# Weights read in steps of four columns, so that each partition loads four adjoining rows of w_out

## The chip, the cores and the metric

The kernel runs on one core of one Trainium2 chip. The metric is the device time of one execution in microseconds (us), lower is better. Engines are named as in the profile: PE is the matrix engine (PEld is its loading of weights), DVE the vector engine, ACT the scalar engine, POOL the general engine that also issues the loads which convert a type, and SP the engine that only issues transfers.

## The reference

Linear attention with a cosine weighting, and behind it a two-layer network with a squared ReLU. `q`, `k`, `v` are (8, 8, 576, 64) in float32, `moe_w_in` is (512, 2048), `moe_w_out` is (2048, 512).

```python
def phi(x, c, s):
    r = np.maximum(x, 0.0)
    return np.concatenate([r * c, r * s], axis=-1)
q_p = phi(q, cos_w, sin_w)
k_p = phi(k, cos_w, sin_w)
kv = np.einsum('bhsf,bhsd->bhfd', k_p, v)
z = np.sum(k_p, axis=2)
num = np.einsum('bhsf,bhfd->bhsd', q_p, kv)
den = np.einsum('bhsf,bhf->bhs', q_p, z)[..., None] + 1e-06
x = (num / den).transpose(0, 2, 1, 3).reshape(4608, 512)
h = x @ w_in
r = np.maximum(h, 0.0)
out = (r * r) @ w_out
```

The sum over the 2048 hidden units in the second product may be taken in any order, as long as the same unit is meant on both sides.

## The kernel before

Each of the eight batches has 576 tokens: four tiles of 128 (512 tokens, one "block" of the network) and a tail of 64. The eight tails make a ninth block. All products are in bfloat16 with sums in float32. For a block `m` the first product makes `gT[m]`, hidden units on the partitions (16 groups `hb` of 128 units), 512 tokens along the free side; ACT takes the ReLU out of PSUM (on-chip accumulator) and DVE squares. The second product takes slices of `gT` as weights and streams `w2sb`.

The weights stay on chip. `w1sb` is a tile of 128 partitions by 4 by 2048 (`kb`, hidden unit); `w2sb` is 128 by 16 by 512 (`hb`, output column). POOL loads each in four quarters: `load_w1(i, 4)` (L294 issues it) brings 512 columns of `w_in`, `load_w2(i, 4)` (L301) brings 512 rows of `w_out`. Both convert float32 to bfloat16 on the way. The quarters are called w1(0) to w1(3) and w2(0) to w2(3) below.

Where `w1sb` is used as weights of a matmul:

- `first_mm` (L712): the first product of block 0, 160 matmuls, in a hand-made order `FIRST_S` that begins with the quarter w1(0) for the first two token tiles; 64 of them are 128 wide, the others 256 wide;
- `unit_half` and `unit_mm` (L568, L584): the first product of block 1;
- `in_product` (L661): blocks 2 to 8, where the first product is made of seven half-size products in place of eight (a Strassen-like scheme). It takes quarters of `w1sb` or sums of them, `w1t[1]`, `w1t[2]`, `w1t[4]`, and `w1t[3]`, which lies in the place of a part of `w1sb`. DVE makes these sums in `w1_sum` (L619).

The second product is `first_out` (L737) for block 0, `out_pair` (L751) for block 1 and `product` (L850) for the others.

The order of everything is worked out on the host before the program is built. Each piece of work is handed to `Plan.add` with an engine, an assumed duration, what it reads and writes, and a due time; `Plan.order` then places the pieces in one list, and this list is the order in which instructions are written down. Each engine runs its own part of it strictly in that order. The reads and writes given to `Plan.add` only make this list. The waits that the chip really carries out are derived a second time, when the program is built: the framework looks at which bytes of a tile each instruction reads or writes, and in which order the instructions were written down. The loads of weights are given to the plan with fixed start times, 2.6 us apart:

```python
    plan_pool(2.6, lambda: load_w1(0, 4), [("w1", 0)])
    for i in range(1, 4):
        plan_pool(2.6, lambda i=i: load_w1(i, 4), [("w1", i)])
```

so in the written order the first matmuls of block 0 stand between the issues of w1(1) and w1(2), and more of them between w1(2) and w1(3). POOL's queue goes on, in this order, with q(1), w2(0), k(1), the tail of k(1), w2(1), v(1), the tail of v(1), w2(2), w2(3), where q(1), k(1), v(1) are the inputs of batch 1. The later batches are loaded by SP.

Of the kernel before, what the change touches and what calls it, by code (L numbers as in the profile page):

```python
# [158 lines left out]
def kernel(  # L159
# [10 lines left out]
    P = nc.NUM_PARTITIONS  # L170
# [118 lines left out]
    w1sb = wpool.tile([P, KB, DFF], BF16, name="w1sb")  # L289
    w2sb = wpool.tile([P, HB, DM], BF16, name="w2sb")  # L290

    def load_w1(i, n):
# [3 lines left out]
            in_=moe_w_in[:, f0:f1].rearrange("(kb p) f -> p kb f", p=P),  # L296
        )

    def load_w2(i, n):
        h0, h1 = i * HB // n, (i + 1) * HB // n  # L300
        nc.gpsimd.dma_start(  # L301
            out=w2sb[:, h0:h1, :],
            in_=moe_w_out[h0 * P : h1 * P, :].rearrange("(hb p) f -> p hb f", p=P),
        )


# [27 lines left out]
    def xT_of(b):  # L334
        return home(mlp, [P, 2, KB, W], "xT", b % 2)
# [225 lines left out]
    def x_block(m, kb):  # L561
        if m < B:
            return xT_of(m)[:, :, kb, :]
        return xT8[:, kb, :, :]

    def unit_half(m, hb, to, i):
        for kb in range(KB):
            nc.tensor.matmul(  # L568
                out=bank[to][:, i * W : (i + 1) * W],
                lhsT=w1sb[:, kb, hb * P : (hb + 1) * P],  # L570
                rhs=xT_of(m)[:, i, kb, :],
                start=(kb == 0),
                stop=(kb == KB - 1),
            )

    def unit_mm(m, hb, to):
        out_ = bank[to][:, :]
        rhs0 = x_block(m, 0)
        if m < B:
            out_ = out_.rearrange("p (i c) -> p i c", i=2)  # L580
        else:
            out_ = out_.rearrange("p (b c) -> p b c", b=B // 2)
        for kb in range(KB):
            nc.tensor.matmul(  # L584
                out=out_,
                lhsT=w1sb[:, kb, hb * P : (hb + 1) * P],
                rhs=x_block(m, kb),
                start=(kb == 0),
                stop=(kb == KB - 1),
            )  # L590
# [65 lines left out]
    def in_product(m, n, u, to):  # L656
        fresh, of = IN_PRODUCTS[n]
        lhs, rhs = of(m)
        for s in range(2):
            for kb in range(2):  # L660
                nc.tensor.matmul(  # L661
                    out=bank[to][:, s * W : (s + 1) * W],
                    lhsT=lhs[:, kb, (2 * u + s) * P : (2 * u + s + 1) * P],
                    rhs=rhs[:, kb, :],
                    start=(fresh and s == 0 and kb == 0),
                    stop=(kb == 1),
                    skip_group_check=True,
                )
# [37 lines left out]
    def first_mm(s, a, c0, step):  # L706
        half, hq = s // 4, s % 4
        for c in (c0,):
            for i in (2 * a, 2 * a + 1):
                hb = hq * 4 + i  # L710
                for kb in range(KB):
                    nc.tensor.matmul(  # L712
                        out=bank[2 * (FIRST_S.index(s) % 2) + i // 2][:, i % 2 * W + c : i % 2 * W + c + step],
                        lhsT=w1sb[:, kb, hb * P : (hb + 1) * P],
                        rhs=xT_of(0)[:, half, kb, c : c + step],
                        start=(kb == 0),
                        stop=(kb == KB - 1),
                    )
# [268 lines left out]
    def plan_unit(m, hb, to, due, halves=False):  # L987
        w1 = [("w1", hb // 4)]
        if halves:
            for h in range(2):  # L990
                add("PE", 4 * 0.1092, lambda h=h: unit_half(m, hb, to, h),
                    r=w1 + [("xT", m % 2, j) for j in (2 * h, 2 * h + 1)], w=[("bank", to)], due=due,
                    name=f"u{m}.{hb}.{h}")
        else:
            r = [("xT", m % 2, j) for j in range(J)] if m < B else [("xT8", i) for i in range(B // 2)]
            add("PE", 4 * 0.2158, lambda: unit_mm(m, hb, to), r=r + w1, w=[("bank", to)], due=due,
                name=f"u{m}.{hb}")
        add("ACT", cost("ACT", 512, "psum"), lambda: unit_relu(m, hb, to),
            r=[("bank", to)], w=[key for i in range(2) for key in g_keys(m, i, hb // HB2, (hb % HB2,))])
# [28 lines left out]
    def plan_gemm1_7(m, t, dt):  # L1028
# [19 lines left out]
        for u in range(HB2 // 2):  # L1048
# [5 lines left out]
            def prod(n, to):  # L1054
                add("PE", 4 * 0.1092, lambda u=u: in_product(m, n, u, to), r=reads[n], w=[("bank", to)],
                    due=t + (7 * u + STRIDE * c[0] + SHIFT) * dt, name=f"h{m}.{u}.{n}")
                c[0] += 1
# [210 lines left out]
    def plan_first(s):  # L1268
        n, half, hq = FIRST_S.index(s), s // 4, s % 4
        parts = ((0, P), (P, P)) if s in (0, 4) else ((0, W),)  # L1270
        for c0, step in parts:
            js = [2 * half + j for j in range(2) if c0 < (j + 1) * P and j * P < c0 + step]
            for a in range(2):
                to = 2 * (n % 2) + a
                add("PE", 8 * 0.1092 * step / W, lambda a=a, c0=c0: first_mm(s, a, c0, step),
                    r=[("xT", 0, j) for j in js] + [("w1", hq)], w=[("bank", to)], due=TM + (n + (a + c0 / P) / 4) * dt0)
        for a in range(2):
            to = 2 * (n % 2) + a
            add("ACT", 0.48, lambda a=a: first_relu(s, a), r=[("bank", to)],
                w=[("g", 0, half, hb // HB2, hb % HB2) for hb in range(4 * hq + 2 * a, 4 * hq + 2 * a + 2)])  # L1280
        add("DVE", 0.60, lambda: first_square(s),
            w=[("g", 0, half, hb // HB2, hb % HB2) for hb in range(4 * hq, 4 * hq + 4)])
# [14 lines left out]
    for half in range(2):  # L1297
        for i, e in enumerate(("DVE", "ACT")):
            js = slice(2 * i, 2 * i + 2)
            add(e, cost(e, FP, "cast"), lambda half=half, js=js, e=e: first_v(half, js, ENG[e]),  # L1300
                r=[("v", half)], w=[("v0", half, i)])
# [23 lines left out]

    plan_pool(2.6, lambda: load_main("q", 1, nc.gpsimd), [("q", 0), ("q", 1), ("q01",), ("q23",)])
    plan_pool(2.6, lambda: load_w2(0, 4), [("w2", 0)])
    plan_pool(2.75, lambda: load_main("k", 1, nc.gpsimd), [("k", 0), ("k", 1)])
    plan_pool(0.4, lambda: load_tail("k", 1, nc.gpsimd), [("kt", 1)])
    plan_pool(2.7, lambda: load_w2(1, 4), [("w2", 1)])  # L1330
    plan_pool(2.8, lambda: load_main("v", 1, nc.gpsimd), [("v", 0), ("v", 1)])
    plan_pool(0.4, lambda: load_tail("v", 1, nc.gpsimd), [("vt", 1)])
    for i in range(2, 4):
        plan_pool(2.6, lambda i=i: load_w2(i, 4), [("w2", i)])
# [6 lines left out]
    for hb in range(HB):  # L1341
        add("PE", 4 * 0.2158, lambda hb=hb: first_out(hb),
            r=[("g", 0, i, hb // HB2, hb % HB2) for i in range(2)] + [("w2", hb // 4)],
# [11 lines left out]
    for tt in range(J):  # L1355
        e = "ACT" if tt % 2 == 0 else "DVE"
        add(e, cost(e, 512, "psum"), lambda tt=tt, e=e: first_copy(tt, ENG[e]),
            r=[("bank", FIRST_Y[tt])], w=[("y", tt // 2, tt % 2)])
# [102 lines left out]
```

## Time and profile before

| | |
|---|---|
| median of 3 runs | 276.02 us (275.52 to 277.29) |
| profiled execution, its own time | 276.42 us |
| its span from first to last instruction | 274.6 us |
| PE busy | 265.0 us (96%) |
| PEld busy | 215.2 us (78%) |
| DVE busy | 225.9 us (82%) |
| ACT busy | 186.8 us (68%) |
| POOL busy | 15.2 us (6%) |
| mean granted clock of PE | 0.996 |

The busy time of PE is modelled: a matmul of 256 columns is shown as 273 ns long, while a run of them starts one every 109 ns. The span is shorter than the time by 1.8 us, which lie around the program. A line of the timeline gives start, length (both in us), engine, line of the code, operation, the tiles written and read with partitions and elements, and the number of equal instructions put together; in square brackets stands the idle time of the engine ahead of it and what ended that.

### The profile page before, as it was taken

The page shows a single profiled execution, that of the slowest core. Times are in us where ns is not written, and L with a number is a line of the kernel's source. Part 1 is how long each engine was busy: PE and PEld are TensorE (multiplying, and loading weights), DVE is VectorE, ACT ScalarE, POOL GpSimd, SP SyncE. Part 2 cuts the span into 40 slices and gives each one's busy share as a digit, 9 for nine tenths or more (in the row PEclk, how much of TensorE's full clock was granted, in tenths as well). Part 3 has the DMA queues.
Part 4 walks back from the last instruction along what each step waited for, and adds up shares of the span by engine and source line. Part 5 has one row for each costly group of instructions (what it writes and reads, how often), then busy time and mean ns, then how long its engine had stood idle before and what let it go on. Part 6 is the DMA issues. An engine that isn't in the chain of part 4 may idle for free.

```text
span 274.6 us, 6700 instructions
## 1 busy us (share of the span) xinstructions
PE 265.0 (96%) x2698; PEld 215.2 (78%) x2706; DVE 225.9 (82%) x450; ACT 186.8 (68%) x336; POOL 15.2 (6%) x29
## 2 busy tenths in 40 slices
PE   8989999999999999999999999999999999999993
PEld 3669856565478669899998889989988888888882
DVE  1865997947969999999999999999989974888911
ACT  3865671696689899898879997865646763464231
POOL 1563100000000000000000000000000000000022
PEclk9999999999999999999999999999999999999998
DMA  7999999999998979999999999985202100300134
GB/s 213 306 204 276 284 279 284 296 245 297 264 289 255 259 202 282 329 246 168 287 301 241 230 271 253 165 183 181 41 1 96 79 2 0 155 1 2 76 117 115
DMA packets 87006, 53.38 MB, mean 194 GB/s; under 512 B 56928, under 2 KB 83936, under 8 KB 86976
## 3 DMA queue, kind: packets, MB, share of 16 engines
q1 hardware_dynamic: 81504, 44.64, 63.4%
q0 software_dynamic: 5392, 8.26, 13.9%
q8 instruction: 21, 0.34, 0.5%
q10 hardware_dynamic: 80, 0.07, 0.1%
q14 instruction: 9, 0.07, 0.1%
HBM read 36.70 MB, written 9.44 MB: 168 GB/s over the span
## 4 chain that ended last, share of the span: by engine, by line
PE 80%; DMA 8%; DVE 3%; SPq 2%; issue 1%; ACT 1%; POOL 1%; POOLq 0%; DVEq 0%
PE bank L661 31%; PE bank L850 31%; DMA k<-in_k_dram 6%; PE bank L751 4%; PE bank L737 3%; PE abank L387 3%; PE bank L584 3%; PE abank L499 3%; DMA q<-in_q_dram 2%; DVE qp L345 1%; SPq L239 1%; ACT kp L341 1%; PE bank L568 1%; DVE gT L601 1%; SPq L249 1%
## 5 line engine op out<-in xcount | busy, mean ns | idle before, releaser
L661 PEld LDWEIGHTS <-w1sb 128*128 128x128 bf16 x448 | 43.3, 98 | 6.0
L661 PE MATMUL bank<-xT,w1sb 128*128 128x256 bf16 x336 | 47.8, 273 | 0.0
L850 PEld LDWEIGHTS <-gT 128*128 128x128 bf16 x448 | 43.3, 98 | 5.6 <-issue 0.6
L677 ACT ACTIVATE gT<-bank 128x512 bf16<-128x512 f32 x56 | 33.1, 600 | 16.9 <-PE bank L661 15.6
L850 PE MATMUL bank<-w2sb,gT 128*128 128x256 bf16 x336 | 41.9, 273 | 0.6 <-ACT ysb L761 0.6
L684 DVE TENSOR_TENSOR gT<-bank,qpTp 128x512 bf16<-128x512 f32 x56 | 36.7, 686 | 4.7 <-PE bank L661 3.7
L601 DVE TENSOR_TENSOR gT<-gT 128x2048 bf16<-128x2048 bf16 (+1 forms) x32 | 37.7, 1189 | 1.8 <-ACT gT L677 1.5
L1060 ACT COPY bank<-bank 128x512 f32<-128x512 f32 x56 | 31.4, 581 | 7.5 <-PE bank L661 7.0
L850 PEld LDWEIGHTS <-gs 128*128 128x128 bf16 x336 | 32.5, 98 | 3.8
L661 PEld LDWEIGHTS <-w1t 128*128 128x128 bf16 x336 | 31.9, 98 | 4.4
L661 PE MATMUL bank<-qpTp,w1t 128*128 128x256 bf16 x224 | 32.7, 273 | 0.0
L850 PE MATMUL bank<-w2t,gs 128*128 128x256 bf16 x224 | 27.6, 273 | 0.0
L1077 ACT COPY qpTp<-bank 128x512 f32<-128x512 f32 x28 | 16.1, 589 | 9.8 <-PE bank L661 5.6
L523 DVE TENSOR_TENSOR x<-abank,rden 128x512 bf16<-128x512 f32 x30 | 20.7, 691 | 1.0
L1148 DVE TENSOR_TENSOR ysb<-bank,y 128x512 f32<-128x512 f32 x14 | 9.7, 690 | 9.6 <-PE bank L850 8.3
L661 PE MATMUL bank<-xT,w1t 128*128 128x256 bf16 x112 | 16.8, 272 | 0.0
L661 PE MATMUL bank<-zeros,w1sb 128*128 128x256 bf16 x112 | 16.6, 273 | 0.0
L712 PE MATMUL bank<-xT,w1sb 128*128 128x256 bf16 (+1 forms) x160 | 15.5, 251 | 0.6 <-ACT gT L722 0.6
L341 ACT ACTIVATE qp<-q,sin_col 128x512 bf16<-128x512 f32 x23 | 16.1, 717 | 0.0
L784 POOL DMA_DIRECT2D out_dram<-ysb x4 | 2.4, 613 | 237.6 <-ACT ysb L1152 235.2
L341 ACT ACTIVATE kp<-k,cos_col 128x512 bf16<-128x512 f32 x18 | 12.6, 715 | 4.3 <-DMA k<-in_k_dram 4.3
L751 PE MATMUL bank<-w2sb,gT 128*128 128x512 bf16 x60 | 14.9, 379 | 0.5 <-DVE gT L601 0.3
(118 smaller groups left out, 423.5 us busy)
## 6 DMA issues: line engine op xcount, KB each, us to landing
out_dram<-ysb SPq DMA_DIRECT2D x16, 512.0 KB, 3.9
q<-in_q_dram SPq DMA_DIRECT2D x14, 512.0 KB, 6.3
v<-in_v_dram SPq DMA_DIRECT2D x14, 512.0 KB, 6.0
k<-in_k_dram SPq DMA_DIRECT2D x12, 512.0 KB, 6.7
w1sb<-in_moe_w_in_dram POOLq DMA_DIRECT2D x4, 512.0 KB, 9.3
w2sb<-in_moe_w_out_dram POOLq DMA_DIRECT2D x4, 512.0 KB, 17.5
k<-in_k_dram SPq DMA_DIRECT2D x1, 1024.0 KB, 5.6
q<-in_q_dram POOLq DMA_DIRECT2D x1, 1024.0 KB, 11.9
```

Of the source, the lines that this page charges most:

```text
L341: eng.activation(out=dst[ps, :, lo : lo + D], in_=src[ps], func=ACTF.Relu, scale=col[ps])
L523: nc.vector.tensor_tensor(out=x[:, a:z], in0=n4[:, :, :, 0:D].rearrange("p b (k l) d -> p b k l d", l=2), in1=rden[:, a:z] .rearrange("p b ...
L601: nc.vector.tensor_tensor(out=g, in0=g, in1=g, op=ALU.mult)
L661: nc.tensor.matmul(out=bank[to][:, s * W : (s + 1) * W], lhsT=lhs[:, kb, (2 * u + s) * P : (2 * u + s + 1) * P], rhs=rhs[:, kb, :], start= ...
L677: nc.scalar.activation(out=g_pair(m, i, j, u), in_=bank[to][:, :].rearrange("p (s c) -> p s c", s=2), func=ACTF.Relu,)
L684: nc.vector.tensor_tensor(out=g_pair(m, i, j, u), in0=bank[to][:, :].rearrange("p (s c) -> p s c", s=2), in1=in_five(u).rearrange("p (s c) ...
L712: nc.tensor.matmul(out=bank[2 * (FIRST_S.index(s) % 2) + i // 2][:, i % 2 * W + c : i % 2 * W + c + step], lhsT=w1sb[:, kb, hb * P : (hb + ...
L751: nc.tensor.matmul(out=bank[LAST_Y[s_]][:, :], lhsT=gT_of(m)[:, hb, tt * P : (tt + 1) * P], rhs=w2sb[:, hb, :], start=(hb == 0), stop=(hb ...
L850: nc.tensor.matmul(out=bank[to][:, s * DM2 : (s + 1) * DM2], lhsT=lhs[:, hb, s * P : (s + 1) * P], rhs=rhs[:, hb, :], start=(fresh and hb ...
L1060: add("ACT", psum, lambda: nc.scalar.copy(out=bank[b][:, :], in_=bank[a][:, :]), r=[("bank", a)], w=[("bank", b)])
L1077: add("ACT", psum, lambda u=u, Y=Y: nc.scalar.copy(out=in_five(u), in_=bank[Y][:, :]), r=[("bank", Y)], w=five)
L1148: lambda: nc.vector.tensor_tensor(out=y_view(m, i, cc), in0=half_bank(a), in1=five_of(m)[:, :, :], op=ALU.add),
```

## The change

`load_w2` gives each partition four rows of `w_out` that lie one behind the other, one stretch of 8 KB in memory, where before it took four rows that lie 128 rows apart, four stretches of 2 KB. With that, the hidden unit at partition `p` of group `hb` is another one: within each quarter of 512 units it is unit `4 p + hb mod 4`. So that the first product makes the same units in the same places, its weights are taken from `w1sb` in steps of four columns: `cols(hb)` is a slice with a step of 4 elements (8 bytes) in place of 128 adjoining columns. The loading of `w1sb`, the sums of the weights, and the number, shapes and order of the instructions stay.

```diff
+    RUN = 4
+
+    def cols(hb):
+        c0 = hb // RUN * RUN * P + hb % RUN
+        return slice(c0, c0 + RUN * (P - 1) + 1, RUN)
+
     def load_w2(i, n):
         h0, h1 = i * HB // n, (i + 1) * HB // n
+        assert h1 - h0 == RUN
         nc.gpsimd.dma_start(
             out=w2sb[:, h0:h1, :],
-            in_=moe_w_out[h0 * P : h1 * P, :].rearrange("(hb p) f -> p hb f", p=P),
+            in_=moe_w_out[h0 * P : h1 * P, :].rearrange("(p r) f -> p r f", r=RUN),
         )
...
 # unit_half, unit_mm, first_mm (L568, L584, L712)
-                lhsT=w1sb[:, kb, hb * P : (hb + 1) * P],
+                lhsT=w1sb[:, kb, cols(hb)],
...
 # in_product (L661)
-                    lhsT=lhs[:, kb, (2 * u + s) * P : (2 * u + s + 1) * P],
+                    lhsT=lhs[:, kb, cols(2 * u + s)],
```

More of the change, by code (lines that the diff above doesn't have):

```diff
@@ L585, in unit_mm @@
                 out=out_,
-                lhsT=w1sb[:, kb, hb * P : (hb + 1) * P],
+                lhsT=w1sb[:, kb, cols(hb)],
                 rhs=x_block(m, kb),
@@ L713, in first_mm @@
                         out=bank[2 * (FIRST_S.index(s) % 2) + i // 2][:, i % 2 * W + c : i % 2 * W + c + step],
-                        lhsT=w1sb[:, kb, hb * P : (hb + 1) * P],
+                        lhsT=w1sb[:, kb, cols(hb)],
                         rhs=xT_of(0)[:, half, kb, c : c + step],
```

## The prediction

> **What bounds the kernel now.** I read the busy shares first, then the costliest groups, the timeline of the first 25 us, the landing of the loads, and the instruction lists of the two builds side by side.
>
> ```profile
> PE 265.0 (96%) x2698; PEld 215.2 (78%) x2706; DVE 225.9 (82%) x450; ACT 186.8 (68%) x336; POOL 15.2 (6%) x29
> L661 PEld LDWEIGHTS <-w1sb 128*128 128x128 bf16 x448 | 43.3, 98 | 6.0
> L661 PE MATMUL bank<-xT,w1sb 128*128 128x256 bf16 x336 | 47.8, 273 | 0.0
> ```
>
> PE runs nearly from end to end, so any microsecond in which PE stands still is lost: nothing later has slack to give it back. Weight loads lie beside the matmuls (a 256-wide matmul starts every 109 ns, the load is shown as 98 ns).
>
> The timeline of PE and POOL in the first stage, where the weights arrive:
>
> ```profile
> 10.60 3.15 POOL L294 DMA_DIRECT2D w1sb<-in_moe_w_in_dram  x4
> 17.67 0.61 PE L712 MATMUL bank<-xT,w1sb 128*128 128x128 bf16 x8
> 18.12 0.61 PE L480 MATMUL bank<-ident,qp 128*128 128x128 bf16 x8
> 18.56 0.61 PE L712 MATMUL bank<-xT,w1sb 128*128 128x128 bf16 x8
> 19.01 0.41 PE L499 MATMUL abank<-kvz,qpTp 128*128 128x65 bf16 x8
> 19.25 2.10 PE L712 MATMUL bank<-xT,w1sb 128*128 128x128 bf16 x24
> 21.66 1.91 PE L712 MATMUL bank<-xT,w1sb 128*128 128x256 bf16 x16
> 22.70 0.70 POOL L249 DMA_DIRECT2D vt<-in_v_dram  x1 [1.38 <-DMA w1sb<-in_moe_w_in_dram]
> 25.29 0.76 POOL L301 DMA_DIRECT2D w2sb<-in_moe_w_out_dram  x1 [1.89 <-DMA w1sb<-in_moe_w_in_dram]
> ```
>
> POOL issues all four quarters of w_in back to back from 10.60. PE starts L712 at 17.67, while w1(2) and w1(3) are still under way; POOL's later waits end at 22.70 and 25.29 because these two have just landed. Landing by issue, from the view of the transfers in 10.5 to 11.3 us and in 11.3 to 12.1 us (last column: median us from issue to landing):
>
> ```profile
> w1sb<-in_moe_w_in_dram POOLq DMA_DIRECT2D x1, 512.0 KB, 5.8
> w1sb<-in_moe_w_in_dram POOLq DMA_DIRECT2D x2, 512.0 KB, 7.1
> ```
>
> w1(0): 10.60 + 5.8 = 16.4. The second row is the mean of 5.8 and w1(1)'s own, so 8.4; issued at 11.49, w1(1) lands at 19.9. w1(3) lands at about 25.0, just ahead of the wait that ends at 25.29.
>
> **The change, part by part.**
>
> *The order* of instructions is the same on all five engines. *The waits are not.* With a step of four, the framework no longer sees that `cols(hb)` of one quarter stays clear of the other quarters. The build of the changed kernel has, new:
> - PE: the second weight load of the first L712 group (17.67) waits for w1(1); the second load of the next one (18.56) waits for w1(2); the second load of the group at 21.66 waits for w1(3). Before, PE met these waits only where the quarter was needed.
> - POOL: the issue of w1(2) waits until PE has finished the first L712 group; the issue of w1(3) until PE has finished the run that starts at 19.25. Before, neither waited.
> - Near 71 us: `w1_sum(3)` on DVE waits for four L661 matmuls, and a weight load two matmuls on waits for that sum.
>
> So two loads that were issued ahead now stand behind PE, and PE behind them; q(1), w2(0), k(1) and all else in POOL's queue stand behind both.
>
> *Step 1, first stall.* The group of 17.67 goes on at 19.9: seven matmuls 56 ns apart (eight L480 take 0.45) and the length of the last, 0.22, end it at 20.5.
>
> *Step 2, w1(2).* Issued at 20.6. How long does such a load take alone? Upper bound 5.8 (w1(0), beside other loads until about 12.5). Lower bound: the 2.6 us that one quarter lands behind another (22.70 to 25.29), plus the 2.4 us of the shortest POOL transfer of the page (128 KB), less 0.3 for its own data at that pace: 4.7. I take 5.5, nearer to the row of the same transfer. It lands at 26.1; PE has stood since about 21.1.
>
> *Step 3, the clock.* Rows on what PE does after standing still (windows; behind PE's and the other engines' busy times come granted clock, share and rate of the transfers; then weight loads of the start):
>
> ```profile
> 269.00:270.00 1.00, 0.92 (x9) 0.58 (x6) 0.00 (x0) 0.42 (x2) 0.26 (x1) 1.00 0.77 176
> 272.00:273.00 1.00, 0.00 (x0) 0.00 (x0) 0.00 (x0) 0.00 (x0) 0.00 (x0) 0.84 0.50 147
> 273.00:274.60 1.60, 0.00 (x0) 0.00 (x0) 0.00 (x0) 0.00 (x0) 0.00 (x0) 0.50 0.00 0
> 5.43 0.15 PEld L369 LDWEIGHTS <-zeros 128*128 128x128 bf16 x1 [0.27 <-issue]
> 5.86 0.15 PEld L369 LDWEIGHTS <-zeros 128*128 128x128 bf16 x1 [0.28 <-issue]
> 6.29 3.20 PEld L369 LDWEIGHTS <-zeros 128*128 128x128 bf16 x15 [0.28 <-issue]
> ```
>
> The last matmul ends at 269.9 and the clock halves at 272.7, 2.8 us later. At the start PE works from 1.2 at one load per 0.43 us, and from 6.3 at one per 0.21: 5.1 us of work at half speed. A stall of 5 us is over the 2.8, so PE comes back at half speed for about 5.1 us. [...]
>
> *Step 4, w1(3).* From the freed load to the end of the run at 19.25 + 2.10 = 21.35, PE needed 2.7 us (18.6 to 21.35), 2.4 of it matmuls; at half speed 5.0. So POOL issues w1(3) at 31.1, and it lands at 36.6. PE stands for another 4 to 5 us ahead of the group that stood at 21.7.
>
> *Step 5, the loss at this point:* 36.6 - 21.7 = 14.9 us. The clock is low once more for 5.1 us; the timeline shows PE without a gap from 21.7 to 36.5 (L712, then L737), so half of that is lost: 2.6 us.
>
> *Step 6, what comes back.* w1(3) lands 11.6 us later than before (36.6 against 25.0) and the queue behind it follows at its old spacing, so q(1), k(1), w2 are late by 11.6, PE by 14.9 to 17.5. They are no longer what PE waits for. The gap of 0.56 us ahead of PE's L712 at 37.07 (ACT late, because k(1) landed at 33.95) goes: -0.6.
>
> *Step 7, near 71 us:*
>
> ```profile
> 71.42 1.04 PE L661 MATMUL bank<-xT,w1sb 128*128 128x256 bf16 x8
> 71.67 1.22 DVE L619 TENSOR_TENSOR w1sb<-w1sb 128x2048 bf16<-128x2048 bf16 x1
> 74.48 1.04 PE L751 MATMUL bank<-w2sb,gT 128*128 128x512 bf16 x4 [0.29 <-DVE gT L601]
> ```
>
> The sum starts when four of the eight L661 are done (72.0) and ends at 73.3; the other matmuls end their starts at 73.8, eight L751 at 216 ns follow to 75.5, where before PE went on at 74.48 after a wait that is then covered: +1.1 us.
>
> *Step 8, w2's longer stretches.* A quarter lands about 2.6 us behind the one before. Were w2 faster, the gain would be covered, since by step 6 these loads lead PE by 3 us or more; at most the 0.6 already counted. POOL's issue (0.77 us) is off the path. Without that cover it could give some tenths.
>
> *Step 9, weights read with a step.* No row shows one. Lower end: 65-wide matmuls start every 33 ns (40 of L387 in 1.31 us), so a packed load needs no more than that of PE; a stepped one like it is hidden at no cost. Upper ends: if the shown 98 ns were all occupied, the 64 matmuls that are 128 wide lose 98 - 56 = 42 ns each, 2.7 us; if a load took four packed ones (four times the bytes are spanned), 132 ns, 904 matmuls of 256 lose 23 ns and the 64 lose 76: 25.7 us. The nearest row is the other form of load: 16 of 64 columns start within 0.22 us (L499, 100.05), 15 ns each, 30 for 128 columns. I take nothing.
>
> *Sum:* 14.9 + 2.6 - 0.6 + 1.1 = 18.0, on the profiled execution's own 276.4 (span 274.6 and 1.8 around it): 294.4. Its own time is 0.4 over the median of 276.0; the forecast for the median is 294.0.
>
> **Rivals.**
> 1. *The clock does not fall* in these stalls. For: the profile's clock row reads 1.00 wherever PE had gaps of 1 us. Against: 2.8 us at the end. Then step 4 is 2.7 us (28.8), w1(3) lands at 34.4, the loss is 12.7 and no 2.6: 276.4 + 12.7 + 0.5 = 289.6; with 4.7 us a load, 288.
> 2. *Stepped weights are slow as well:* 2.7 to 25.7 us more, 297 to 320. For: 78% of the span has weights loading. Against: the pitches of step 9. [...]
> 3. *Not slower:* the new waits are over when an engine reaches them, and only longer stretches of w2 remain: the 0.6 of step 6, 275.8. It needs w1(2) to land within 0.3 us of an issue that can't come before 18.3, and the shortest transfer took 2.4; from a wait of a further microsecond it turns round.
>
> **How the numbers follow.** Forecast 0.64, rival 1 0.15, rival 2 0.18, rival 3 0.03. The range goes from rival 1 with loads of 4.7 us and an earlier w1(1), 287, to rival 2's smaller prices above the forecast with loads of 5.8, 300; the far end of rival 2 and rival 3 are left out. Changes within 1% are about what a measurement here can't tell from none: slower 0.97, same 0.02, faster 0.01.
>
> **What would show it.** Right: POOL's four L294 in three pieces (about 10.6, 20.6, 31); PE gaps ahead of L712 ended by w1sb landings, 2, 5 and 4 to 5 us long; a clock below 1 in 20 to 42 us; from 80 us on the same pitch. Wrong: L661 starts further apart than 109 ns (rival 2), a full clock (rival 1), or L294 still in one piece (rival 3).

## The result and the profile after

The changed kernel takes 293.76 us (median of 4 runs, 292.69 to 294.11), where the kernel before took 275.77 us beside it (4 runs, 275.22 to 277.29): 1.065 times as long, with a 95% interval of 1.062 to 1.067. The profiled execution's own time is 294.11 us, its span 292.3 us, 17.7 us over the 274.6 before. The nine new lines of code shift what follows `load_w1`: L661 of before is L670 now, L712 is L721, L480 is L489, L737 is L746, L568 is L577, L619 is L628, L751 is L760; `load_w1` stays L294.

The page of the changed kernel, with the busy shares, the granted clock in 40 slices of 7.3 us each (in tenths), and the groups of the first product:

```profile
PE 270.6 (93%) x2698; PEld 230.0 (79%) x2706; DVE 225.6 (77%) x450; ACT 186.7 (64%) x336; POOL 14.4 (5%) x29
PEclk9975769999999999999999999999999999999999
L670 PEld LDWEIGHTS <-w1sb 128*128 128x128 bf16 x448 | 48.6, 114 | 3.0 <-DVE w1sb L628 1.5
L721 PE MATMUL bank<-xT,w1sb 128*128 128x256 bf16 (+1 forms) x160 | 20.9, 299 | 11.4 <-DMA w1sb<-in_moe_w_in_dram 11.4
```

The last line has the loss in it: 11.4 us in which PE's first product waits for landings of `w_in`, where before none of PE's waits was for `w_in`. The clock row falls in slices three to six (14.6 to 43.8 us) and nowhere else. The weight loads are shown 114 ns long in place of 98, but a 256-wide matmul still starts every 109 ns: eight L670 matmuls stand in the timeline with a length of 1.04 us, as eight L661 did.

The timeline of PE and POOL in the first stage and up to where block 0 is done (the square brackets are the idle time ahead and what ended it):

```profile
10.41 1.70 POOL L294 DMA_DIRECT2D w1sb<-in_moe_w_in_dram  x2
19.41 0.94 PE L721 MATMUL bank<-xT,w1sb 128*128 128x128 bf16 x7 [1.86 <-DMA w1sb<-in_moe_w_in_dram]
20.64 0.74 POOL L294 DMA_DIRECT2D w1sb<-in_moe_w_in_dram  x1 [8.54 <-PE bank L721]
26.06 0.94 PE L721 MATMUL bank<-xT,w1sb 128*128 128x128 bf16 x7 [4.75 <-DMA w1sb<-in_moe_w_in_dram]
31.15 0.74 POOL L294 DMA_DIRECT2D w1sb<-in_moe_w_in_dram  x1 [9.76 <-PE bank L721]
36.67 3.39 PE L721 MATMUL bank<-xT,w1sb 128*128 128x256 bf16 x15 [4.77 <-DMA w1sb<-in_moe_w_in_dram]
53.81 1.04 PE L721 MATMUL bank<-xT,w1sb 128*128 128x256 bf16 x8
```

Read it as a ladder. POOL issues two quarters and then waits 8.54 us for PE; PE waits 4.75 us for the quarter that POOL could issue only then; POOL waits 9.76 us for PE again, and PE 4.77 us for the last quarter. Before, the four issues stood in one line (10.60, x4). On each rung of the last two, PE resumes 5.4 and 5.5 us after the issue: the time of one load alone.

Windows of the same stretch (busy time of PE, PEld, DVE, ACT, POOL; then granted clock, share and GB/s of the transfers):

```profile
18.00:20.00 2.00, 0.59 (x6) 0.59 (x7) 0.29 (x1) 0.00 (x0) 0.00 (x0) 0.53 0.12 17
26.00:28.00 2.00, 1.94 (x23) 1.94 (x24) 0.46 (x3) 0.60 (x1) 0.00 (x0) 0.50 0.00 0
32.00:34.00 2.00, 0.00 (x0) 0.00 (x0) 0.79 (x2) 0.00 (x0) 2.00 (x3) 1.00 0.50 55
34.00:36.00 2.00, 0.00 (x0) 0.00 (x0) 0.00 (x0) 0.00 (x0) 2.00 (x4) 0.79 1.26 215
40.00:42.00 2.00, 2.00 (x22) 2.00 (x21) 0.42 (x1) 0.60 (x1) 0.40 (x1) 0.50 1.03 305
```

In 26 to 28 and in 40 to 42 us PE is at work almost without a break, at half the clock.

Where the 17.7 us of span arose is seen from how much later the same work starts in the changed kernel:

| work | before | after | later by |
|---|---|---|---|
| group that waits for w1(3) (L712, L721) | 21.66 | 36.67 | 15.0 |
| eight transposes behind the half clock (L480, L489) | 28.91 | 46.38 | 17.5 |
| last eight of block 0 (L712, L721) | 37.07 | 53.81 | 16.7 |
| first L661, L670 of the next product | 71.42 | 88.13 | 16.7 |
| the eight L661, L670 after the eight L751, L760 | 75.35 | 92.99 | 17.6 |
| end of the span | 274.6 | 292.3 | 17.7 |

(The 36.67 is the first matmul that waited, the second of its group; the group's first, at 31.51, had not.) The first two rows are the ladder and its half clock, the third gives 0.7 us back, the fifth is the place where `w1_sum(3)` stands:

```profile
88.13 0.71 PE L670 MATMUL bank<-xT,w1sb 128*128 128x256 bf16 x5
88.77 1.23 DVE L628 TENSOR_TENSOR w1sb<-w1sb 128x2048 bf16<-128x2048 bf16 x1 [0.31 <-PE bank L670]
90.05 0.52 PE L670 MATMUL bank<-xT,w1sb 128*128 128x256 bf16 x3 [1.21 <-DVE w1sb L628]
92.99 1.04 PE L670 MATMUL bank<-qpTp,w1t 128*128 128x256 bf16 x8
```

The eight L670 are cut into five and three, and between them PE waits 1.21 us for DVE's sum, which itself could start only when some of these matmuls had read the old weights.

### The profile page after: what moved, and what is told of

It reads as the page before. It is cut to its first block, busy times and chain, and to the rows that moved or that the text cites. A ratio compares the mean times of both kernels' runs of the same rounds, so it can differ in the third digit from the quotient of the medians.

```text
span 292.3 us, 6700 instructions
## 1 busy us (share of the span) xinstructions
PE 270.6 (93%) x2698; PEld 230.0 (79%) x2706; DVE 225.6 (77%) x450; ACT 186.7 (64%) x336; POOL 14.4 (5%) x29
## 3 DMA queue, kind: packets, MB, share of 16 engines
q0 software_dynamic: 3856, 8.26, 12.4%
## 4 chain that ended last, share of the span: by engine, by line
PE 85%; DMA 7%; issue 4%; POOL 1%; DVE 1%; SPq 1%; ACT 0%; POOLq 0%
PE bank L670 30%; PE bank L859 29%; PE bank L721 5%; PE bank L746 5%; PE bank L760 5%; DMA w1sb<-in_moe_w_in_dram 5%; PE bank L593 4%; PE abank L396 3%; PE abank L508 3%; DMA v<-in_v_dram 2%; PE bank L577 1%; PE bank L489 1%; POOL w1sb L294 1%; PE bank L554 0%; DVE w1sb L628 0%
## 5 line engine op out<-in xcount | busy, mean ns | idle before, releaser
L670 PEld LDWEIGHTS <-w1sb 128*128 128x128 bf16 x448 | 48.6, 114 | 3.0 <-DVE w1sb L628 1.5
L670 PE MATMUL bank<-xT,w1sb 128*128 128x256 bf16 x336 | 48.0, 273 | 1.2 <-DVE w1sb L628 1.2
L686 ACT ACTIVATE gT<-bank 128x512 bf16<-128x512 f32 x56 | 33.0, 600 | 16.9 <-PE bank L670 15.6
L693 DVE TENSOR_TENSOR gT<-bank,qpTp 128x512 bf16<-128x512 f32 x56 | 36.6, 682 | 4.7 <-PE bank L670 3.8
L670 PEld LDWEIGHTS <-w1t 128*128 128x128 bf16 x336 | 36.0, 114 | 1.1
L670 PE MATMUL bank<-qpTp,w1t 128*128 128x256 bf16 x224 | 32.8, 273 | 0.0
L721 PE MATMUL bank<-xT,w1sb 128*128 128x256 bf16 (+1 forms) x160 | 20.9, 299 | 11.4 <-DMA w1sb<-in_moe_w_in_dram 11.4
L721 PEld LDWEIGHTS <-w1sb 128*128 128x128 bf16 x160 | 17.0, 128 | 13.6 <-DMA w1sb<-in_moe_w_in_dram 12.2
L731 ACT ACTIVATE gT<-bank 128x512 bf16<-128x512 f32 x16 | 9.1, 596 | 20.2 <-PE bank L721 20.2
L526 DVE TENSOR_SCALAR den<-abank 128x8 f32<-128x8 f32 x34 | 5.4, 159 | 19.4 <-PE abank L508 15.9
L670 PE MATMUL bank<-xT,w1t 128*128 128x256 bf16 x112 | 16.8, 273 | 0.0
L670 PE MATMUL bank<-zeros,w1sb 128*128 128x256 bf16 x112 | 16.6, 273 | 0.0
```

Source lines behind the costliest of these rows:

```text
L670: nc.tensor.matmul(out=bank[to][:, s * W : (s + 1) * W], lhsT=lhs[:, kb, cols(2 * u + s)], rhs=rhs[:, kb, :], start=(fresh and s == 0 and ...
L686: nc.scalar.activation(out=g_pair(m, i, j, u), in_=bank[to][:, :].rearrange("p (s c) -> p s c", s=2), func=ACTF.Relu,)
L693: nc.vector.tensor_tensor(out=g_pair(m, i, j, u), in0=bank[to][:, :].rearrange("p (s c) -> p s c", s=2), in1=in_five(u).rearrange("p (s c) ...
L721: nc.tensor.matmul(out=bank[2 * (FIRST_S.index(s) % 2) + i // 2][:, i % 2 * W + c : i % 2 * W + c + step], lhsT=w1sb[:, kb, cols(hb)], rhs ...
```

## The experiments

The theory is that of the prediction: the stepped reads of one large tile make the framework put in waits that the data don't need; they tie two loads and PE to each other, and with the idle time the clock halves (0.50 in the windows above). The rivals are that the stepped weight loads cost time themselves, and that the other half of the change, `w2`'s longer stretches, does something. Each experiment takes one of these away or has it alone.

**split_tiles: the change kept, the tile taken apart.** Each quarter of `w_in` gets its own tile, so that a stepped slice can't reach into another quarter. The sums of the weights become two instructions each.

```diff
-    w1sb = wpool.tile([P, KB, DFF], BF16, name="w1sb")
+    w1q = [wpool.tile([P, KB, FQ], BF16, name=f"w1sb{i}") for i in range(4)]
-            out=w1sb[:, :, f0:f1],
+            out=w1q[i][:, :, :],
-                lhsT=w1sb[:, kb, cols(hb)],
+                lhsT=w1q[hb // RUN][:, kb, cols(hb % RUN)],
...
-        nc.vector.tensor_tensor(out=w1t[n], in0=in0, in1=in1, op=op)
+        for x in range(2):
+            nc.vector.tensor_tensor(out=to(x), in0=in0(x), in1=in1(x), op=op)
```

> Both parts of the change stay (steps of four, four adjoining rows of w_out), but each quarter of w_in has a tile of its own, so that no load or matmul waits for another quarter; each of the four weight sums is written as two instructions. If the added waits are the whole loss: POOL's four loads of w_in in one piece from about 10.5 us, the clock at full speed in 18 to 42 us, no PE wait on a landing of w_in over 0.3 us, and the time of before plus 0 to 1 us for the four more DVE instructions: 275.5 to 277.5 us. If stepped weights cost by themselves: the loss stays in the stages of L712 and in_product; 2.7 us (279) if the 64 matmuls of 128 columns wait for loads that are now shown as 114 to 128 ns, more if the 256-wide ones start over 109 ns apart.

Measured: 275.82 us (12 runs) against 275.6 for the kernel before (23 runs), a ratio of 1.0003 (0.9987 to 1.002); span 274.0 us, mean clock 0.999. POOL's and PE's timeline, and the group of the stepped loads:

```profile
10.52 3.23 POOL L295 DMA_DIRECT2D w1sb<-in_moe_w_in_dram  x4
36.34 1.04 PE L726 MATMUL bank<-xT,w1sb 128*128 128x256 bf16 x8
```

```profile
L675 PEld LDWEIGHTS <-w1sb 128*128 128x128 bf16 x448 | 48.7, 113 | 1.6
```

The four issues are in one piece again, and PE nowhere waits for `w_in`. The loads are as stepped as in the changed kernel, and shown as long (113 ns), yet the loss is gone. So the loss is in the waits, and stepped weights cost nothing that this comparison could see; nor do they where matmuls are 128 columns wide, since runs of 8 and 24 L726 take 0.45 and 2.11 us as before. The second line answers to the 37.07 of before: its 0.56 us of idle time ahead is gone.

**steps_alone and rows_alone: the two halves of the change.** The first is the changed kernel with the old `load_w2`; the second is the kernel before with the new one. In both, the hidden units of the two products no longer correspond; the work is the same in amount.

```diff
# steps_alone, against the changed kernel
-            in_=moe_w_out[h0 * P : h1 * P, :].rearrange("(p r) f -> p r f", r=RUN),
+            in_=moe_w_out[h0 * P : h1 * P, :].rearrange("(hb p) f -> p hb f", p=P),
# rows_alone, against the kernel before
-            in_=moe_w_out[h0 * P : h1 * P, :].rearrange("(hb p) f -> p hb f", p=P),
+            in_=moe_w_out[h0 * P : h1 * P, :].rearrange("(p r) f -> p r f", r=4),
```

> The changed kernel with the old load of w_out (rows 128 apart); the steps of four stay, so the hidden units of the two products do not match. Waits theory: all of the loss, 293 to 295 us, with the same three PE stalls. If the load of w_out has a part in it, the time moves off 293.8 by that part.

> Before, with only the load of w_out changed to four adjoining rows; the weights of the first product stay packed, so the hidden units of the two products do not match. Waits theory: 275.2 to 276.4 us, no different from before, since w2 leads PE. If the longer stretches are worth something: k(1) lands 0.2 to 0.6 us earlier than 33.95 and the time falls by as much. If the load of w_out were part of the loss: several us slower.

Measured: steps_alone 293.94 us (292.55 to 295.47), ratio 1.0655 (1.0612 to 1.0698), with 12.3 us of PE's waits for `w_in` in three pieces. rows_alone 275.4 us (275.21 to 276.84, 12 runs), ratio 0.9992 (0.9975 to 1.0009). All of the loss is in the steps. The longer stretches do work in the queue: q0 carries 3856 packets in the changed kernel where it carried 5392, and in rows_alone k(1) lands 0.9 us sooner after the first weight load's issue (22.5 us in place of 23.4), so that PE's wait of 0.56 us goes. The 0.9 is more than the 0.2 to 0.6 that was expected. In the time this can't be told from nothing.

**loads_first: the ladder without its rungs.** The issues of all four quarters are written down ahead of the first matmul. POOL then has nothing of PE's to wait for; PE's own false waits stay, and become one wait for the last of the four landings.

```diff
-    plan_pool(2.6, lambda: load_w1(0, 4), [("w1", 0)])
+    plan_pool(2.6, lambda: [load_w1(i, 4) for i in range(4)], [("w1", 0)])
     for i in range(1, 4):
-        plan_pool(2.6, lambda i=i: load_w1(i, 4), [("w1", i)])
+        plan_pool(2.6, lambda: None, [("w1", i)])
```

> The changed kernel with all four loads of w_in written down ahead of the first matmul that uses w_in. POOL no longer waits for PE; PE waits once, for all four quarters. If it is the chain of PE and POOL waiting for each other in turn that costs: one PE stall from 17.4 to about 25.0 (7.5 us), half clock for some 5 us after it (2.5 us), the sum near 71 us (1.1), less 0.6: 286 to 288 us. If POOL's waits do not matter: 293 to 295 us.

Measured: 285.91 us (285.09 to 286.26), ratio 1.0353 (1.0315 to 1.0391); a tenth under the expected range. POOL's loads stand in one piece at 10.32, and PE's timeline has a single stall:

```profile
24.68 0.91 PE L721 MATMUL bank<-xT,w1sb 128*128 128x128 bf16 x7 [7.03 <-DMA w1sb<-in_moe_w_in_dram]
```

So the 18 us are two things: 293.76 - 285.91 = 7.9 us because POOL's issues wait for PE (with the half clock that this adds), and some 10 us because PE waits for quarters that it doesn't yet need. The second is made up of the 7.0 us, half of the 5.7 us at half clock that follow (2.9), the 0.9 at the sum, less the 0.7 that comes back: 10.1, against a measured 10.3 (285.91 against 275.6).

**filled: the clock by itself.** The waits stay, but PE gets matmuls on zeros ahead of the waiting groups (7, 20 and 20 of them, into banks that are free then), so that it never stands long. They add work and change no result that is used.

```diff
+    FILL = {(0, 1, 0): (7, 0), (0, 1, P): (20, 0), (1, 0, 0): (20, 1)}
...
     def first_mm(s, a, c0, step):
         half, hq = s // 4, s % 4
+        fill(*FILL.get((s, a, c0), (0, 0)))
```

> The changed kernel with matmuls on zeros written ahead of the three waiting groups of L712 (7, 20 and 20, each 512 columns wide), so that PE works while it would stand; nothing reads their results. If the halved clock is part of the loss: granted clock 1.00 from 15 to 45 us, POOL's third w_in load issued about 2.4 us earlier relative to the second (the work between the stalls at full speed), no half-speed stretch after the last stall (2.6 us): 288 to 290 us. If the clock costs nothing: 293 to 295 us, or more, by the added matmuls.

Measured: 289.14 us (288.64 to 290.18), ratio 1.0497 (1.0478 to 1.0516). PE still stands 0.35, 0.88 and 2.02 us, and the clock stays full from 15 to 45 us; one of the windows:

```profile
24.00:28.00 4.00, 3.12 (x43) 2.57 (x42) 1.06 (x3) 1.14 (x2) 0.00 (x0) 1.00 0.35 57
```

Doing more work makes the changed kernel faster by 293.76 - 289.14 = 4.6 us. It acts twice: the work after the last stall runs at full speed (the 15 matmuls behind it take 1.83 us in place of 3.39), and the third and fourth issue stand 8.3 us apart (20.30 and 28.59) in place of 10.5, because the matmuls between them do too. The price of the clock may be somewhat higher than this difference: in filled the last load took 6.6 us from its issue (28.59) to PE's resumption (35.21), in place of 5.5, and no run shows why.

**first_plain: the place at the sum by itself.** Of the product that reads `w1sb` just ahead of `w1_sum(3)`, the first two groups take packed columns, so that they read only the quarter they need. These groups compute other hidden units.

```diff
-                    lhsT=lhs[:, kb, cols(2 * u + s)],
+                    lhsT=lhs[:, kb, (2 * u + s) * P : (2 * u + s + 1) * P]
+                    if (m, n) == (2, 1) and u < 2
+                    else lhs[:, kb, cols(2 * u + s)],
```

> The changed kernel, but the first two groups of in_product (block 2, first product, the eight matmuls ahead of the third weight sum) take packed columns, so their hidden units do not match. The wait between these matmuls and the sum near 71 us (88 us in the changed kernel) goes. By the prediction's step 7: 1.1 us less than the changed kernel, 292.4 to 293.0 us, and no PE wait on w1_sum. If that stall was covered by the wait behind it: 293.5 to 294 us.

Measured: 292.8 us (290.8 to 294.57, 6 runs), ratio 1.063 (1.06 to 1.066). The runs spread over 3.8 us, so the median's distance of 1.0 us from the changed kernel says little, and so does its place in the expected range. The trace says more:

```profile
85.75 1.04 PE L670 MATMUL bank<-xT,w1sb 128*128 128x256 bf16 x8
89.67 1.04 PE L670 MATMUL bank<-qpTp,w1t 128*128 128x256 bf16 x8
```

The eight are in one piece, and the next eight follow 3.92 us later; in the changed kernel it was 4.86 (88.13 to 92.99), in the kernel before 3.93 (71.42 to 75.35). The false wait at the sum costs 0.94 us.

**bursts: what a stepped load needs of PE when little hides it.** In the kernel before, the last 8 of the 28 matmuls on zeros at the start are replaced by four bursts of 16 matmuls of only 64 columns, with weights that are packed (L372) or read in steps of two (L376), four (L380) and eight (L384).

```diff
+        warm(20)
+        packed(16)       # lhsT=probe[:, 0:P]
+        step_two(16)     # lhsT=probe[:, 0:255:2]
+        step_four(16)    # lhsT=probe[:, 0:509:4]
+        step_eight(16)   # lhsT=probe[:, 0:1017:8]
```

> Before, with the last 8 of the 28 warming matmuls replaced by four bursts of 16 matmuls of 64 columns on zeros, whose weights are packed, or in steps of two, four and eight columns, each burst on a line of its own. It measures what a stepped load occupies. If a stepped load costs only its added length (114 against 98 ns, overlapped): all bursts start one matmul every 30 to 35 ns. [...] Time within 1 us of before.

Measured (one run: 275.64 us), PE's timeline:

```profile
7.75 0.63 PE L372 MATMUL abank<-zeros,gT 128*128 128x64 bf16 x16
8.22 0.63 PE L376 MATMUL abank<-zeros,gT 128*128 128x64 bf16 x16
8.69 0.70 PE L380 MATMUL abank<-zeros,gT 128*128 128x64 bf16 x16
9.22 1.14 PE L384 MATMUL abank<-zeros,gT 128*128 128x64 bf16 x16
```

From start to start of the bursts, 16 matmuls take 0.47, 0.47 and 0.53 us: 29, 29 and 33 ns each. The last burst's length of 1.14 us, less the 0.16 us that its last matmul is shown to last beyond its turn in the first burst (0.63 - 0.47), gives about 61 ns; the next matmul in the timeline starts at 10.19, 0.97 us after the burst, which gives the same. So a step of four bf16 needed at most 33 ns per load of 128 columns, far below the 109 ns of a 256-wide matmul and the 56 ns of a 128-wide one; a step of eight needed some 60. The first three bursts are at or under the 30 to 35 ns of a load that costs only its added length, the fourth does not; why, no run shows.

**wide_steps: steps of eight where PE is busiest.** split_tiles, with the weights of three of the products (336 loads) read in steps of eight from the tiles of the sums; these products compute other hidden units.

```diff
# against split_tiles, for products 5, 6 and 3
+    def wide_cols(h):
+        return slice(h, h + 8 * (P - 1) + 1, 8)
...
-    lhsT=lhs((2 * u + s) // RUN)[:, kb, cols((2 * u + s) % RUN)],
+    lhsT=lhs[:, kb, wide_cols(2 * u + s)],
```

> The split kernel, with the weights of the three products that use sums of w_in taken in steps of eight columns (16 bytes), the others in steps of four; the hidden units of these products do not match. If loads in steps of eight stay hidden beside 256-wide matmuls (109 ns apart): 275.4 to 276.4 us, and their shown length tells the slope: 98 packed, 114 at four, 130 to 140 at eight. If they take over 109 ns of the loading path: 336 loads times the excess, several us slower.

Measured: 276.33 us (275.91 to 276.94, 10 runs), ratio to the kernel before 1.0032 (1.0022 to 1.0043); the loads are shown longer than a 109 ns matmul turn:

```profile
L678 PEld LDWEIGHTS <-w1t 128*128 128x128 bf16 x336 | 38.8, 145 | 1.0
```

If 145 ns were occupied, 336 loads would lose (145 - 109) x 336 = 12 us. Between half a microsecond (276.33 against split_tiles' 275.82, which ran on another occasion) and 0.9 us (against the 275.44 of the kernel before beside it) is there, so the shown length of a weight load is not its price.

## Why the prediction was right

The forecast was 294.0 us, and 293.76 was measured; the loss of 18.0 on the profiled execution came out as 17.7 of span. By its steps:

- *The order and the waits.* Right. POOL's four L294 stand in three pieces, and PE's three stalls end with landings of `w1sb`. That the stepped reads of a single tile are the cause, and not the step as such, is shown by split_tiles. How the framework works out the reach of a stepped slice was not looked at; only the waits it made were. What stands ahead of the prediction says that it looks at which bytes an instruction reads; for a stepped slice the waits it made cover quarters of which not a byte is read.
- *Step 1.* PE went on at 19.4, not 19.9, but at half speed: its seven matmuls took 0.94 us. The two errors cancelled, and POOL's issue came at 20.64 (forecast 20.6).
- *Step 2.* 5.4 and 5.5 us for a load alone, forecast 5.5. It was chosen between 4.7 and 5.8 by the row of the same transfer, and that row came nearer.
- *Step 3.* The clock did halve, but the rule behind the forecast was wrong. It took 2.8 us of standing for the fall and 5.1 us of work for the return, each from one instance. In the traces of the changed kernel, loads_first and first_plain the clock changed at instants that lie 3.41 us or whole multiples of it apart, and fell 0.6 to 5.2 us after the last matmul (worked out in the last section). Here it fell some 0.6 us after the last matmul ahead of the first stall (17.55; the mean of 0.53 in 18 to 20 us means half clock from about 18.1 on), in a stall of 1.86 us that the forecast took for harmless. The return took 5.7 and 5.3 us of work. That this is so near the 5.1 is in part luck: in first_plain, whose code is the same in this stage, the clock stayed full in the first stall and the returns took 2.8 and 3.4 us. Its profiled execution of 290.8 us, with the 0.9 of step 7 added, is 2.4 us under the changed kernel's 294.11.
- *Step 4.* 26.06 to the issue at 31.15 is 5.1 us, forecast 5.0; the last landing at 36.67, forecast 36.6.
- *Step 5.* 15.0 us and 17.5 - 15.0 = 2.5, forecast 14.9 and 2.6.
- *Step 6.* Forecast -0.6, measured -0.7: the gap ahead of the last L721 is gone, and nothing behind the late loads in POOL's queue made PE wait. rows_alone and split_tiles, in which PE is not late, lose the gap too, and k(1) lands 0.9 us earlier in both (in split_tiles at 33.06). steps_alone, in which PE is late and `w_out` is loaded as before, has no such gap either: no L721 waits for ACT among its waits of 0.3 us and more. So PE's lateness takes the gap away by itself, as forecast, and the longer stretches alone would have done it as well.
- *Step 7.* Forecast 1.1, measured 0.93, by the table and by first_plain. The mechanism was the one described. Of the small error, 0.1 is in the forecast's own sum (75.5 - 74.48 is 1.0, not 1.1); the rest is that PE had issued five of the eight matmuls ahead of its wait, where the forecast left four of them behind it.
- *Step 8.* Nothing that can be measured, as forecast: rows_alone has 0.9992.
- *Step 9.* Nothing, as forecast: 114 ns shown, hidden. The choice fell on the nearest row, the pitch of 15 ns for 64 columns, 30 for 128; the burst with a step of four gives 33. The two upper bounds, which took the shown length or the spanned bytes for the price, were both wrong, the second by four times.

Rival 1 (a full clock) gave 289.6 on the profiled execution, and filled, in which the clock is full, takes 290.18 there (median 289.14). Its third and fourth issue came at 20.30 and 28.59, where the rival's sum has 20.6 and 28.8, but its last landing at 35.21 in place of 34.4. So the price of the clock in that sum was right within a microsecond, and only its condition was not met. Rival 2 fell with split_tiles, rival 3 with the ladder in the timeline.

## What to carry to other kernels

The change of an access pattern cost nothing that could be measured in the engine that carries it out (split_tiles: 275.82 us against 275.6) and 18 us in what the framework derived from it: when slices of a tile that is loaded in parts become stepped, compare the waits of the two builds, and give each part that lands by itself a tile of its own. A load whose issue waits for the engine that waits for the load showed up in this profile as issues torn apart, each ended by the consumer; the price per rung was the whole time of a transfer alone (5.4 and 5.5 us from issue to PE's resumption). The stalls cost more than their length, through the clock: 4.6 of 18 us, by filled.

## What was not expected of the hardware

**The clock changed at instants 3.41 us, or whole multiples of it, apart.** From the last matmul to the half clock it took 2.8 us at the end of the span before, about 0.6 us at the first stall after and 3.2 at the last (31.91 to 35.16), about 2.5 us in loads_first, and 1.1 and 5.2 us in first_plain. From resumed work back to the full clock it took 5.7 and 5.3 us in the changed kernel, 5.7 in loads_first, and 2.8 and 3.4 in first_plain. These spans scatter, but the instants of the changes don't. Two of the changed kernel's, 31.75 and 35.16 us, lie 3.41 us apart; if its stretch is cut into pieces of that length, no piece has a mixed clock (behind each window stand its length and PE's busy time; the third value from the end is the clock):

```profile
14.68:18.10 3.42, 1.80 (x24) 1.12 (x20) 2.26 (x8) 1.87 (x4) 0.00 (x0) 1.00 1.21 201
18.10:21.51 3.41, 1.90 (x16) 1.63 (x16) 0.19 (x1) 0.27 (x1) 0.74 (x1) 0.50 0.05 7
21.51:24.92 3.41, 0.00 (x0) 0.00 (x0) 0.00 (x0) 0.74 (x1) 0.00 (x0) 0.50 0.88 127
24.92:28.34 3.42, 2.28 (x26) 2.28 (x27) 0.80 (x3) 0.60 (x1) 0.00 (x0) 0.50 0.17 27
28.34:31.75 3.41, 3.41 (x29) 2.68 (x26) 1.33 (x4) 1.19 (x2) 0.60 (x1) 0.50 0.00 0
31.75:35.16 3.41, 0.16 (x1) 0.00 (x0) 1.02 (x2) 0.00 (x0) 3.41 (x6) 1.00 0.72 103
35.16:38.58 3.42, 1.91 (x10) 1.32 (x11) 0.00 (x0) 0.19 (x1) 2.49 (x4) 0.50 1.10 358
38.58:41.99 3.41, 3.41 (x27) 3.01 (x26) 1.12 (x2) 1.01 (x2) 0.55 (x1) 0.50 1.05 273
41.99:45.40 3.41, 3.41 (x41) 3.40 (x40) 1.41 (x3) 2.14 (x5) 0.00 (x0) 1.00 1.06 321
```

The changes at 18.10, 31.75, 35.16 and 41.99 us lie four, one and two pieces apart. Two other runs with stalls agree. The mean clock of loads_first is 0.55 in 20 to 22 us and 0.89 in 30 to 32, that of first_plain 0.63 in 20 to 26, 0.80 in 26 to 32, 0.90 in 32 to 36 and 0.78 in 36 to 42. With one change between 1.00 and 0.50 in each of these windows, the changes stand at 20.2 and 30.4 in loads_first (three pieces) and at 21.6, 28.4, 35.2 and 38.6 in first_plain (two, two, one). Those of loads_first lie 1.3 us off the changed kernel's (20.2 against 18.10 + 3.41 = 21.51), though PE's first matmul starts at 1.2 us in both; so the instants are not counted from the start of the work. In 31.75 to 35.16 us the changed kernel's clock reads 1.00, though PE is busy for only 0.16 us of that piece.

In these runs the clock rose behind pieces in which PE was busy for 2.8 us (first_plain, from 25.55 to 28.4) and 3.41 us (the changed kernel, twice), and not behind pieces with 2.3 us (loads_first, 24.68 to 27.0) or, in the changed kernel, 2.28 us and less. What made it fall is less plain: in the changed kernel it fell behind pieces with 1.80 and 0.16 us of work, but in first_plain it stayed full behind one with 1.6 us (PE is busy from 28.4 to 30.02 and stands up to 31.8). The first stall came out differently in these two: in first_plain (1.78 us) the clock stayed full, behind a piece (14.7 to 18.1) with 1.8 to 1.9 us of work; in the changed kernel (1.86 us) it fell. What decides this, no run shows. The six runs of first_plain fit a clock that differs from run to run: their times rise from 290.8 to 294.57 us as their mean clock falls from 0.980 to 0.963.

**The shown length of a weight load said little of its price.** 98 ns packed, 113 to 118 with a step of four, 145 to 171 with a step of eight, while the turn they needed in the bursts was at most 29, 33 and about 60 ns.
